# Five pieces of the query-weight gradient, placed by a load count, in a two-block attention backward kernel

## The chip, the cores and the metric

The kernel runs on one core of one Trainium2 chip. The metric is the device time of one execution in microseconds (us). A core has a matrix engine (TensorE, PE in the profile, its weight loads PEld), a vector engine (VectorE, DVE), a scalar engine (ScalarE, ACT), GpSimd (POOL), SyncE (SP), which issues all DMAs here, and 16 DMA engines. Matmuls write to PSUM, which the kernel uses as eight banks of 128 x 2 KB; VectorE or ScalarE copies ("evacuates") a bank to SBUF.

## The reference

Two attention blocks, A and B, each with its own x, caches and weights; the output is their results side by side, and all gradients for a given grad_out are returned too.

```
B, Sq, D = 8, 96, 640;  H, Sk, Dh = 32, 512, 128          # per block, all bf16
q = (x @ wq) by heads;  p = softmax(q @ k_cache^T * Dh**-0.5)
o = p @ v_cache;        out = o.reshape(B, Sq, H*Dh) @ wo
return concat(out_A, out_B), and by vjp: dx, dk_cache, dv_cache, dwq, dwo of each block
```

## The kernel before

**Ticks.** Block A's 32 heads come first, then block B's. One tick is one (head, batch) pair: 8 ticks a head, 256 a block, 512 in all. Each (head, batch) pair goes through eight steps, each one or two ticks behind the other (table OFF), so one tick holds a step of each of several pairs: scores into S_ps and their row maximum negm on VectorE (L298, L300), the exponential E_sb on ScalarE (L310), the normalised P_sb on GpSimd (L329), its transpose PT_sb, the output and its copy into OD (L359 to L378), dV (L389), dP and dl (L417, L419), dS on VectorE (L421), dK (L432), and the transposes of dS and dQ (L340, L346). OD holds, for seven heads, the transposed output OT_h and the transposed query gradient dQT_h.

**Work once a head.** Beside that each head has pieces of its own, put into ticks by the table HK, counted from the head's first tick: pB at -3 (transposes of wo and wq), pC at -2 to 0 (Q and dO), pD at 1 and 2 (their transposes), qA0 at 18 (transposes the output into Onat; evacuated by ScalarE), qA1 at 17 (transposes dQ into dQnat; by VectorE), qB at 19 and 20 (two halves of dwo), and qD. qD computes dwq for two heads at a time, so it runs for odd heads alone: D is cut into DC = 5 chunks of 128 rows, and each chunk is six matmuls of 256 columns over the tokens (L490) from dQnat, which holds the dQ of both heads. Before, two chunks lie in tick 18, two in tick 19 and one in tick 21 of the odd head, counted from that head's first tick, and qD_st stores the result one tick after the last. dQnat and dwq_sb have one buffer each.

**Work once a group.** After every 5 (or 4, or 2) heads, gU multiplies their outputs by wo, and their dQ by wq (o_ps, L514), spread over some 15 ticks. Ticks of other heads have none.

**What sets the order.** An Emitter collects (tick, slot, function) and calls the functions sorted by tick, slot and order of adding. Within a tick the loads come first (slots 0 to 2), then the steps of the pairs, then the work of the heads (SL_HEAD, 90), then the groups' (95). qD is added at SL_HEAD + 2, so behind qA, pD (90) and qB (91) of its tick. A framework orders the instructions of each engine once, at build time, from this order as a priority (the scores, the exponential and the normalisation get a higher one), and sets the semaphores. Each engine then runs its instructions in that order. All PSUM tiles share one pool of eight banks (tag "bank"): whoever allocates waits until an earlier tile's evacuation is done. DMAs that are pinned stay in the order in which they were emitted.

```
HK = dict(pA=-10, pA2=-9, pB=-3, ..., qA0=18, qA1=17, qB=[19, 20], qD=[(18, 0, 2), (19, 2, 4), (21, 4, 5)])
for (k_, c_lo, c_hi) in hk["qD"]:
    if c_lo < DC and h % 2 == 1:
        em.add(c0t + k_, SL_HEAD + 2, qD(h, c_lo, min(c_hi, DC)))
```

In an odd head's count, the following even head's ticks 17, 18, 19, 20 and 21 are 25, 26, 27, 28 and 29.

Of the kernel before, what the change touches and what calls it, by code (L numbers as in the profile page):

```python
# [15 lines left out]
class Emitter:  # L16
    def __init__(self):
        self.items = []
        self.n = 0

    def add(self, tick, slot, fn):
        self.items.append((tick, slot, self.n, fn))
        self.n += 1

    def run(self):
        self.items.sort(key=lambda x: (x[0], x[1], x[2]))
# [14 lines left out]
SL_HEAD = 90  # L41
SL_GRP = 95
SL_SETUP = 96

OFF = dict(ldk=-5, ldv=-4, kt=-3, vt=0, s2=3, s3=3, s4=4, s5=5, s6=6, s7=7, s8=8)
HK = dict(pA=-10, pA2=-9, pB=-3, pC0=[-2, 0], pC1=[-1, 0], pD1=1, pD0=2, qA0=18, qA1=17, qB=[19, 20], qD=[(18, 0, 2), (19, 2, 4), (21, 4, 5)])
EV = dict(pB0="act", pB1="dve", pC00="act", pC01="act", pC10="act", pC11="dve", pD0="dve", pD1="dve", qA0="act", qA1="dve", qB0="act", qB1="dve", qD="dve", gU="act")
GSPREAD0 = 9
PRIO_OFF = 2000
GSPREAD1 = 9  # L50
SLOTS = dict(LOAD=0, S2A=5, S2B=5.5, S1=6, S8=10, S7=20, S5=30, S4=40, S6=50, S3A=52, S3B=53, S5B=54, HEAD=SL_HEAD, GRP=SL_GRP)
# [2 lines left out]
def build_block(tc, em, tick0, blk, x, kc, vc, wq, wo, g_all, out_all, dx, dk, dv, dwq, dwo, ident, ones, pools, HG=6, first=True, groups=None):  # L54
    nc = tc.nc
    B, Sq, D = x.shape
    _, H, Sk, Dh = kc.shape
# [4 lines left out]
    DC = D // 128  # L62
# [142 lines left out]
    def pB(h):  # L205
        def f():
            st = HS[(blk, h)]
            woT_ps = bank([128, DC * 128], BF16, "woT_ps")
            for c in range(DC):
                nc.tensor.transpose(woT_ps[:, c * 128:(c + 1) * 128], st["wo_h"][:, c * 128:(c + 1) * 128], ident[:])  # L210
            woT_h = hd.tile([128, DC * 128], BF16, name="woT_h", bufs=1)
            evac(EV["pB0"], woT_h[:], woT_ps[:])
            st["woT_h"] = woT_h
            wqT_ps = bank([128, DC * 128], BF16, "wqT_ps")
            for c in range(DC):
                nc.tensor.transpose(wqT_ps[:, c * 128:(c + 1) * 128], st["wq_h"][:, c, :], ident[:])
            wqT_h = hst.tile([128, D], BF16, name="wqT_h")
            evac(EV["pB1"], wqT_h[:], wqT_ps[:])
            st["wqT_h"] = wqT_h
            st["slot"] = (blk * H + h) % OD.shape[2]  # L220
            st["OT_h"] = OD[:, 0, st["slot"]]
            st["dQT_h"] = OD[:, 1, st["slot"]]
            st["QT_h"] = hd.tile([128, T], BF16, name="QT_h")
            st["dOT_h"] = hd.tile([128, T], BF16, name="dOT_h")
        return f

    def pC(h, which, si):
        def f():
            st = HS[(blk, h)]
            (t0, w) = tsplits[si]  # L230
            if which == 0:
                dst = st["QT_h"]
                lhs = lambda c: st["wq_h"][:, c, :]
                rhsT = S["xT"]
                sc = scale
            else:
                dst = st["dOT_h"]
                lhs = lambda c: st["woT_h"][:, c * 128:(c + 1) * 128]
                rhsT = S["gT"]
                sc = None  # L240
            q_ps = bank([128, w], F32, "q_ps")
            for c in range(DC):
                nc.tensor.matmul(q_ps[:], lhs(c), rhsT[:, c, t0:t0 + w], start=(c == 0), stop=(c == DC - 1))  # L243
            evac(EV["pC%d%d" % (which, si)], dst[:, t0:t0 + w], q_ps[:], sc)
        return f
# [34 lines left out]
    def c_s1(h, b):  # L280
        def f():
            st = CS[(blk, h, b)]
            kT_ps = bank([128, Sk], BF16, "kT_ps")
            for c in range(KC):
                nc.tensor.transpose(kT_ps[:, c * 128:(c + 1) * 128], st["K_sb"][:, c, :], ident[:])
            KT = wk.tile([128, Sk], BF16, name="KT_pe", bufs=1)
            nc.vector.tensor_copy(KT[:], kT_ps[:])
            st["KT"] = KT[:]
        return f
# [211 lines left out]
    gsplits = dsplits  # L501
# [58 lines left out]
    for g in range(NG):  # L560
        h0 = GH0[g]
        for hh in range(groups[g]):
            h = h0 + hh
            c0t = tick0 + h * B
            if not (first and h == 0):
                em.add(c0t + HK["pA"], SLOTS["LOAD"] + 1.7, pA(h))
                em.add(c0t + HK["pA2"], SLOTS["LOAD"] + 1.7, pA2(h))
            em.add(c0t + HK["pB"], SL_HEAD, pB(h))
            fh = first and h == 0
            p0, p1, d1, d0, late = HK["pC0"], HK["pC1"], HK["pD1"], HK["pD0"], 0  # L570
            if fh:
                p1, d1, d0, late = [3, 3], 3, 4, 7
            elif h == 0:
                p0, p1, d1, d0, late = [-2, 2], [0, 3], 3, 4, 7
            for si in range(NTS):
                em.add(c0t + p0[min(si, 1)], SL_HEAD, pC(h, 0, si))
                em.add(c0t + p1[min(si, 1)], SL_HEAD + late, pC(h, 1, si))
            em.add(c0t + d1, SL_HEAD + (8 if late else 0), pD(h, 1))
            em.add(c0t + d0, SL_HEAD, pD(h, 0))
            for b in range(B):  # L580
                ct = c0t + b
                if b % NB == 0:
                    em.add(tick0 - 12 if first and h == 0 and b == 0 else ct + OFF["ldk"], SLOTS["LOAD"], c_ld(h, b, "K", 7))
                    em.add(ct + OFF["ldv"], SLOTS["LOAD"], c_ld(h, b, "V", 6))
                    if not k_on_pe(h, b):
                        em.add(ct + OFF["kt"], SLOTS["LOAD"] + 1, c_xt(h, b, "KT", 4))
                    em.add(ct + OFF["vt"], SLOTS["LOAD"] + 1, c_xt(h, b, "VT", 4))
                if k_on_pe(h, b):
                    em.add(ct + 2, SLOTS["S1"], c_s1(h, b))
                em.add(ct + OFF["s2"], SLOTS["S2A"], c_s2a(h, b))  # L590
                em.add(ct + OFF["s2"], SLOTS["S2B"], c_s2b(h, b))
                em.add(ct + OFF["s3"], SLOTS["S3A"], c_s3a(h, b))
                em.add(ct + OFF["s3"], SLOTS["S3B"], c_s3b(h, b))
                em.add(ct + OFF["s5"], SLOTS["S5B"], c_s5b(h, b))
                if b % 2 == 1:
                    em.add(ct + OFF["s4"] + 1, SLOTS["LOAD"] + 1.5, c_st(h, b, "v"))
                    em.add(ct + OFF["s7"] + 1, SLOTS["LOAD"] + 1.5, c_st(h, b, "k"))
                em.add(ct + OFF["s4"], SLOTS["S4"], c_s4(h, b))
                for i, o in enumerate(("s8", "s7", "s5", "s4")):
                    SX.setdefault(ct + OFF[o], [None] * 4)[i] = (blk, h, b)  # L600
                em.add(ct + OFF["s6"], SLOTS["S6"], c_s6(h, b))
                em.add(ct + OFF["s7"], SLOTS["S7"], c_s7(h, b))
            hk = HK if first or h < H - 1 else dict(HK, qA0=13, qB=[14, 15], qA1=16, qD=[(19, 0, 2), (19, 2, 4), (19, 4, 5)])
            em.add(c0t + hk["qA0"], SL_HEAD, qA(h, 0))
            for di in range(len(wsplits)):
                em.add(c0t + hk["qB"][di], SL_HEAD + 1, qB(h, di))
            em.add(c0t + hk["qB"][-1] + 1, SLOTS["LOAD"] + 1.6, qB_st(h))
            em.add(c0t + hk["qA1"], SL_HEAD, qA(h, 1))
            for (k_, c_lo, c_hi) in hk["qD"]:
                if c_lo < DC and h % 2 == 1:  # L610
                    em.add(c0t + k_, SL_HEAD + 2, qD(h, c_lo, min(c_hi, DC)))
            if h % 2 == 1:
                em.add(c0t + hk["qD"][-1][0] + 1, SLOTS["LOAD"] + 1.6, qD_st(h))
        cLg = tick0 + (h0 + groups[g] - 1) * B + B - 1
        gs0 = max(3, (GSPREAD0 * groups[g]) // HG)
        gs1 = max(3, (GSPREAD1 * groups[g]) // HG)
        if not first and g == NG - 2:
            gs0, gs1 = 9, 9
        if g == 0:
            em.add(cLg + OFF["s5"] - 2, SL_LOAD, setup_acc)  # L620
        subs = [(0, t, gi) for t in range(TT) for gi in range(len(gsplits))] + [(1, t, gi) for t in range(TT) for gi in range(len(gsplits))]
        n_out = TT * len(gsplits)
        for i, (which, t, gi) in enumerate(subs):
            if which == 0:
                tk = cLg + OFF["s5"] + 2 + (i * gs0) // n_out
            else:
                tk = cLg + OFF["s8"] + 2 + gs0 - 3 + ((i - n_out) * gs1) // n_out
            em.add(tk, SL_GRP, gU(g, which, t, gi))
            if g == NG - 1 and gi == len(gsplits) - 1:
                em.add(tk + 1, SLOTS["LOAD"] + 1.6, gU_st(which, t))  # L630
    pools["c_s45"] = c_s45
    pools["c_s8"] = c_s8
    return tick0 + H * B
# [121 lines left out]
```

## Time and profile before

| | |
|---|---|
| time, median of 3 runs | 1643.09 us (1642.14 to 1643.6) |
| the profiled execution's own time | 1643.09 us |
| its span, first to last instruction | 1641.3 us |
| granted TensorE clock, mean | 1.000 |
| DMA traffic | 454.96 MB, mean 277 GB/s |

How to read it: the profile is of one execution. "Busy" of an engine is the time in which an instruction of it is under way; matmuls are pipelined, and their ends are modelled, so TensorE's busy time is not TensorE at its peak, and two matmuls that follow at once overlap in the rows. A row of the groups has the line, the engine, the operation, out<-in with shapes and the count, then the busy time and the mean of one in ns, then the engine's idle time just before and what ended it. A row of the timeline has the start and the duration in us, and in square brackets the idle time before it with what ended it. A row of the stretches has, for each engine, the busy time and in brackets the number of instructions, then the granted clock, the DMA share and GB/s.

### The profile page before, as it was taken

Reading aid. Unit: us, or ns where it says so; the run is one execution under the profiler, and the core shown is the slowest. Engines: PE = TensorE matmul, PEld = TensorE weight load, DVE = VectorE, ACT = ScalarE, POOL = GpSimd, SP = SyncE. Lnnn points to the kernel's source line nnn. Section 1 sums busy time; section 2 is a strip of 40 time slices with the busy share of each in tenths; the row PEclk is TensorE's granted clock in tenths of the full one; section 3 lists DMA queues with packets and bytes.
Section 4 is the critical chain, followed back from the end, with each engine's and each line's share of the span. In section 5 each row is a group of like instructions: output and inputs, shape, how many; then the busy total and the mean of one; then the engine's idle time right before and its main releaser. Section 6 shows DMA issues by size and latency. Waiting matters only on the chain.

```text
span 1641.3 us, 55280 instructions
## 1 busy us (share of the span) xinstructions
PE 1621.3 (99%) x21048; PEld 1289.1 (79%) x21048; DVE 1268.2 (77%) x2856; ACT 1388.7 (85%) x3518; POOL 526.7 (32%) x1034
## 2 busy tenths in 40 slices
PE   8999999999999999999999999999999999999999
PEld 7887787787787787877878877877877877877876
DVE  6886677778787787788878867878778778777777
ACT  7999897898798797988869998978977978987975
POOL 2333232333233232333323332323322322332332
PEclk9999999999999999999999999999999999999999
DMA  9999999999999999999999999999999999999994
GB/s 266 289 282 294 269 291 291 271 271 292 260 272 293 279 274 271 264 281 285 297 284 292 293 289 279 284 298 260 291 291 258 280 277 282 283 292 259 281 276 146
DMA packets 875626, 454.96 MB, mean 277 GB/s; under 512 B 548192, under 2 KB 875360, under 8 KB 875360
## 3 DMA queue, kind: packets, MB, share of 16 engines
q1 hardware_dynamic: 875360, 451.43, 112.4%
q8 instruction: 165, 2.70, 0.7%
q14 instruction: 101, 0.83, 0.1%
HBM read 161.09 MB, written 159.12 MB: 195 GB/s over the span
## 4 chain that ended last, share of the span: by engine, by line
PE 81%; ACT 10%; DVE 4%; issue 3%; DMA 2%; SPq 0%; POOL 0%; ACTq 0%; DVEq 0%; POOLq 0%
PE q_ps L243 13%; PE o_ps L514 12%; PE dwq_ps L490 6%; PE dP_ps L417 6%; PE dK_ps L432 6%; PE dV_ps L389 5%; PE S_ps L298 5%; PE dst_ps L346 5%; PE dwo_ps L469 4%; PE x_ps L365 4%; PE x_ps L359 4%; PE x_ps L340 4%; ACT E_sb L310 3%; ACT dK_sb L435 2%; PE n_ps L258 2%
## 5 line engine op out<-in xcount | busy, mean ns | idle before, releaser
L329 POOL TENSOR_SCALAR P_sb<-E_sb,rinv 96x512 bf16<-96x512 bf16 x512 | 352.5, 689 | 1087.9 <-DVE rinv L320 1053.6
L310 ACT ACTIVATE E_sb<-S_ps,negm 96x512 bf16<-96x512 f32 x512 | 354.8, 693 | 119.2 <-DVE negm L300 116.8
L421 DVE SCALAR_TENSOR_TENSOR dS_sb<-dP_ps,dl_ps,P_sb 96x512 bf16<-96x512 f32 x512 | 383.6, 749 | 48.9 <-PE dl_ps L419 40.2
L435 ACT ACTIVATE dK_sb<-dK_ps 128x512 bf16<-128x512 f32 x512 | 306.9, 599 | 97.5 <-PE dK_ps L432 96.5
L300 DVE TENSOR_REDUCE negm<-S_ps 96x1 f32<-96x512 f32 x512 | 347.7, 679 | 44.3 <-PE S_ps L298 42.1
L392 ACT ACTIVATE dV_sb<-dV_ps 128x512 bf16<-128x512 f32 x512 | 315.8, 617 | 0.0
L378 ACT ACTIVATE PT_sb<-x_ps 128x384 bf16<-128x384 bf16 x512 | 257.5, 503 | 0.0
L514 PEld LDWEIGHTS <-OD 128*128 128x128 bf16 x1536 | 135.7, 98 | 103.3 <-issue 1.3
L389 PE MATMUL dV_ps<-dOnat_h,P_sb 96*128 96x128 bf16 x2048 | 197.9, 219 | 0.6 <-DVE dOnat_h L160 0.6
L432 PE MATMUL dK_ps<-Qnat_h,dS_sb 96*128 96x128 bf16 x2048 | 197.8, 219 | 0.0
L417 PE MATMUL dP_ps<-VT,dOT_h 128*96 128x512 bf16 x512 | 195.4, 382 | 0.7
L298 PE MATMUL S_ps<-KT,QT_h 128*96 128x512 bf16 x488 | 184.7, 379 | 3.9 <-ACT E_sb L310 2.7
L407 POOL TENSOR_TENSOR prod<-OD,dOT_h 128x96 bf16<-128x96 bf16 x512 | 185.6, 362 | 8.8 <-ACT OD L375 8.2
L348 DVE COPY dST_sb<-dst_ps 128x384 bf16<-128x384 bf16 x512 | 177.2, 346 | 14.0 <-PE dst_ps L346 13.2
L320 DVE RECIPROCAL rinv<-rowsum 96x1 f32<-96x1 f32 x512 | 80.0, 156 | 138.8 <-ACT E_sb L310 134.8
L346 PE MATMUL dst_ps<-ident,dS_sb 96*128 96x96 bf16 x2048 | 171.8, 206 | 4.3 <-ACT PT_sb L378 3.6
L375 ACT ACTIVATE OD<-x_ps 128x192 bf16<-128x192 f32 (+1 forms) x515 | 172.5, 335 | 3.4 <-PE x_ps L340 3.4
L359 PE MATMUL x_ps<-PT_sb,V_sb 128*128 128x96 bf16 x2048 | 172.2, 206 | 0.5 <-ACT PT_sb L378 0.5
L365 PE MATMUL x_ps<-ident,P_sb 96*128 96x96 bf16 x2048 | 171.7, 205 | 0.6 <-POOL P_sb L329 0.3
L340 PE MATMUL x_ps<-dST_sb,K_sb 128*128 128x96 bf16 x2048 | 170.7, 206 | 0.0
L340 PEld LDWEIGHTS <-K_sb 128*128 128x128 bf16 x2048 | 133.7, 98 | 37.1
L514 PE MATMUL o_ps<-wo_h,OD 128*128 128x128 bf16 (+1 forms) x768 | 141.0, 299 | 0.0
(75 smaller groups left out, 3051.9 us busy)
## 6 DMA issues: line engine op xcount, KB each, us to landing
out_dram<-dV_sb SPq DMA_DIRECT2D x256, 256.0 KB, 3.9
out_dram<-dK_sb SPq DMA_DIRECT2D x256, 256.0 KB, 3.6
K_sb<-in_A_k_cache_dram SPq DMA_DIRECT2D x128, 256.0 KB, 4.1
V_sb<-in_A_v_cache_dram SPq DMA_DIRECT2D x128, 256.0 KB, 4.1
K_sb<-in_B_k_cache_dram SPq DMA_DIRECT2D x128, 256.0 KB, 4.2
V_sb<-in_B_v_cache_dram SPq DMA_DIRECT2D x128, 256.0 KB, 4.0
out_dram<-dwo_sb SPq DMA_DIRECT2D x64, 160.0 KB, 3.2
out_dram<-dwq_sb SPq DMA_DIRECT2D x32, 320.0 KB, 3.8
```

The lines of the kernel that those rows point to most:

```text
L298: nc.tensor.matmul(S_ps[:], hs["QT_h"][:, tok], st["KT"], start=True, stop=True)
L300: nc.vector.tensor_reduce(negm[:], S_ps[:], axis=AX.X, op=ALU.max, negate=True)
L310: nc.scalar.activation(E_sb[:], st["S_ps"][:], ACT.Exp, bias=st["negm"][:], scale=1.0, accum_out=rowsum[:])
L329: pinned(nc.gpsimd.tensor_scalar(P_sb[:], st["E_sb"][:], st["rinv"][:], 0.0, op0=ALU.mult, op1=ALU.add))
L340: nc.tensor.matmul(dQT_ps, st["K_sb"][:, c, :], st["dST_sb"][:, c * Sq:(c + 1) * Sq], start=(c == 0), stop=(c == KC - 1))
L389: nc.tensor.matmul(dV_ps[:, c * 128:(c + 1) * 128], P_sb[:, c * 128:(c + 1) * 128], hs["dOnat_h"][:, b * 128:(b + 1) * 128], start=True, s ...
L392: nc.scalar.activation(SB[(blk, h, b // 2, "v")][:, b % 2], dV_ps[:], ACT.Identity, scale=1.0)
L417: nc.tensor.matmul(dP_ps[:], hs["dOT_h"][:, tok], st["VT"], start=True, stop=True)
L421: nc.vector.scalar_tensor_tensor(dS_sb[:], dP_ps[:], dl_ps[:, 0:1], st["P_sb"][:], op0=ALU.subtract, op1=ALU.mult)
L432: nc.tensor.matmul(dK_ps[:, c * 128:(c + 1) * 128], dS_sb[:, c * 128:(c + 1) * 128], hs["Qnat_h"][:, b * 128:(b + 1) * 128], start=True, s ...
L435: nc.scalar.activation(SB[(blk, h, b // 2, "k")][:, b % 2], dK_ps[:], ACT.Identity, scale=1.0)
L514: nc.tensor.matmul(o_ps[:], src[:, t * 128:(t + 1) * 128], rhs, start=(hh == 0), stop=(hh == groups[g] - 1))
```

## The change

Three things change.

- **dwq in pieces of one chunk.** For every odd head but the last of a block, the five chunks of dwq are placed one by one into ticks 18 to 29 of the odd head, at most two in a tick. Two in the same tick form one piece with one evacuation.
- **A load count.** The Emitter's add takes an estimate of the TensorE and ScalarE time (ns) of the work once a head and once a group, and keeps for each tick the sum of TensorE's less 0.8 of ScalarE's. Each chunk goes to the tick whose sum is the smallest so far, and adds 655 to it. The steps of the (head, batch) pairs are in no count, being the same in every tick.
- **dQ of a pair's first head later.** qA1 of the even heads moves from tick 17 to 21 (tick 29 of the odd head before), at SL_HEAD + 3, behind a piece of dwq in the same tick, as dQnat has one buffer.

The last pair of a block keeps its places for dwq. The number of matmuls, their shapes and the data moved stay the same.

```
+        self.load = {}
-    def add(self, tick, slot, fn):
+    def add(self, tick, slot, fn, pe=0, act=0):
         self.items.append((tick, slot, self.n, fn))
         self.n += 1
+        self.load[tick] = self.load.get(tick, 0.0) + pe - ACT_SHARE * act
...
-HK = dict(..., qA0=18, qA1=17, qB=[19, 20], qD=[(18, 0, 2), (19, 2, 4), (21, 4, 5)])
+HK = dict(..., qA0=18, qA1=17, qA1e=21, qDw=(18, 29), qB=[19, 20], qD=[(18, 0, 2), (19, 2, 4), (21, 4, 5)])
+ACT_SHARE = 0.8
...
+            em.add(c0t + HK["pB"], SL_HEAD, pB(h), pe=558, act=713)
...
+                em.add(c0t + p0[min(si, 1)], SL_HEAD, pC(h, 0, si), pe=1090 if si == 0 else 546, act=522 if si == 0 else 420)
+                em.add(c0t + p1[min(si, 1)], SL_HEAD + late, pC(h, 1, si), pe=1090 if si == 0 else 546, act=621 if si == 0 else 0)
+            em.add(c0t + d1, SL_HEAD + (8 if late else 0), pD(h, 1), pe=446)
+            em.add(c0t + d0, SL_HEAD, pD(h, 0), pe=446)
...
+                    em.add(ct + 2, SLOTS["S1"], c_s1(h, b), pe=223)
...
+            em.add(c0t + hk["qA0"], SL_HEAD, qA(h, 0), pe=335, act=820)
             for di in range(len(wsplits)):
+                em.add(c0t + hk["qB"][di], SL_HEAD + 1, qB(h, di), pe=815, act=443 if di == 0 else 0)
-            em.add(c0t + hk["qA1"], SL_HEAD, qA(h, 1))
-            for (k_, c_lo, c_hi) in hk["qD"]:
-                if c_lo < DC and h % 2 == 1:
-                    em.add(c0t + k_, SL_HEAD + 2, qD(h, c_lo, min(c_hi, DC)))
-            if h % 2 == 1:
+            em.add(c0t + (hk["qA1"] if h % 2 == 1 else HK["qA1e"]), SL_HEAD + (0 if h % 2 == 1 else 3), qA(h, 1), pe=335)
+            if h == H - 1:
+                for (k_, c_lo, c_hi) in hk["qD"]:
+                    em.add(c0t + k_, SL_HEAD + 2, qD(h, c_lo, min(c_hi, DC)), pe=655 * (c_hi - c_lo))
                 em.add(c0t + hk["qD"][-1][0] + 1, SLOTS["LOAD"] + 1.6, qD_st(h))
...
+            em.add(tk, SL_GRP, gU(g, which, t, gi), pe=groups[g] * gsplits[gi][1] / 2.4, act=440 if g == 0 else 0)
...
+    for h in range(1, H - 1, 2):
+        c0t = tick0 + h * B
+        ticks = []
+        for _ in range(DC):
+            k_ = min((k for k in range(HK["qDw"][0], HK["qDw"][1] + 1) if ticks.count(k) < 2), key=lambda k: em.load.get(c0t + k, 0.0))
+            em.load[c0t + k_] = em.load.get(c0t + k_, 0.0) + 655
+            ticks.append(k_)
+        ticks.sort()
+        for k_ in sorted(set(ticks)):
+            em.add(c0t + k_, SL_HEAD + 2, qD(h, ticks.index(k_), ticks.index(k_) + ticks.count(k_)))
+        em.add(c0t + ticks[-1] + 1, SLOTS["LOAD"] + 1.6, qD_st(h))
```

More of the change, by code (lines that the diff above doesn't have):

```diff
@@ L45 @@
 OFF = dict(ldk=-5, ldv=-4, kt=-3, vt=0, s2=3, s3=3, s4=4, s5=5, s6=6, s7=7, s8=8)
-HK = dict(pA=-10, pA2=-9, pB=-3, pC0=[-2, 0], pC1=[-1, 0], pD1=1, pD0=2, qA0=18, qA1=17, qB=[19, 20], qD=[(18, 0, 2), (19, 2, 4), (21, 4, 5)])
+HK = dict(pA=-10, pA2=-9, pB=-3, pC0=[-2, 0], pC1=[-1, 0], pD1=1, pD0=2, qA0=18, qA1=17, qA1e=21, qDw=(18, 29), qB=[19, 20], qD=[(18, 0, 2), (19, 2, 4), (21, 4, 5)])
 EV = dict(pB0="act", pB1="dve", pC00="act", pC01="act", pC10="act", pC11="dve", pD0="dve", pD1="dve", qA0="act", qA1="dve", qB0="act", qB1="dve", qD="dve", gU="act")
 GSPREAD0 = 9
+ACT_SHARE = 0.8
 PRIO_OFF = 2000
@@ L567, in build_block @@
                 em.add(c0t + HK["pA2"], SLOTS["LOAD"] + 1.7, pA2(h))
-            em.add(c0t + HK["pB"], SL_HEAD, pB(h))
+            em.add(c0t + HK["pB"], SL_HEAD, pB(h), pe=558, act=713)
             fh = first and h == 0
@@ L575, in build_block @@
             for si in range(NTS):
[L576 to L579, printed above, removed]
+                em.add(c0t + p0[min(si, 1)], SL_HEAD, pC(h, 0, si), pe=1090 if si == 0 else 546, act=522 if si == 0 else 420)
+                em.add(c0t + p1[min(si, 1)], SL_HEAD + late, pC(h, 1, si), pe=1090 if si == 0 else 546, act=621 if si == 0 else 0)
+            em.add(c0t + d1, SL_HEAD + (8 if late else 0), pD(h, 1), pe=446)
+            em.add(c0t + d0, SL_HEAD, pD(h, 0), pe=446)
             for b in range(B):
@@ L588, in build_block @@
                 if k_on_pe(h, b):
-                    em.add(ct + 2, SLOTS["S1"], c_s1(h, b))
+                    em.add(ct + 2, SLOTS["S1"], c_s1(h, b), pe=223)
                 em.add(ct + OFF["s2"], SLOTS["S2A"], c_s2a(h, b))
@@ L603, in build_block @@
             hk = HK if first or h < H - 1 else dict(HK, qA0=13, qB=[14, 15], qA1=16, qD=[(19, 0, 2), (19, 2, 4), (19, 4, 5)])
-            em.add(c0t + hk["qA0"], SL_HEAD, qA(h, 0))
+            em.add(c0t + hk["qA0"], SL_HEAD, qA(h, 0), pe=335, act=820)
             for di in range(len(wsplits)):
-                em.add(c0t + hk["qB"][di], SL_HEAD + 1, qB(h, di))
+                em.add(c0t + hk["qB"][di], SL_HEAD + 1, qB(h, di), pe=815, act=443 if di == 0 else 0)
             em.add(c0t + hk["qB"][-1] + 1, SLOTS["LOAD"] + 1.6, qB_st(h))
-            em.add(c0t + hk["qA1"], SL_HEAD, qA(h, 1))
-            for (k_, c_lo, c_hi) in hk["qD"]:
-                if c_lo < DC and h % 2 == 1:
-                    em.add(c0t + k_, SL_HEAD + 2, qD(h, c_lo, min(c_hi, DC)))
-            if h % 2 == 1:
+            em.add(c0t + (hk["qA1"] if h % 2 == 1 else HK["qA1e"]), SL_HEAD + (0 if h % 2 == 1 else 3), qA(h, 1), pe=335)
+            if h == H - 1:
+                for (k_, c_lo, c_hi) in hk["qD"]:
+                    em.add(c0t + k_, SL_HEAD + 2, qD(h, c_lo, min(c_hi, DC)), pe=655 * (c_hi - c_lo))
                 em.add(c0t + hk["qD"][-1][0] + 1, SLOTS["LOAD"] + 1.6, qD_st(h))
@@ L627, in build_block @@
                 tk = cLg + OFF["s8"] + 2 + gs0 - 3 + ((i - n_out) * gs1) // n_out
-            em.add(tk, SL_GRP, gU(g, which, t, gi))
+            em.add(tk, SL_GRP, gU(g, which, t, gi), pe=groups[g] * gsplits[gi][1] / 2.4, act=440 if g == 0 else 0)
             if g == NG - 1 and gi == len(gsplits) - 1:
                 em.add(tk + 1, SLOTS["LOAD"] + 1.6, gU_st(which, t))
+    for h in range(1, H - 1, 2):
[9 more added lines that the diff above has]
+        em.add(c0t + ticks[-1] + 1, SLOTS["LOAD"] + 1.6, qD_st(h))
     pools["c_s45"] = c_s45
```

## The prediction

> **What bounds the kernel now.** I read the page first: its busy shares, the clock and the chain.
>
> ```profile
> span 1641.3 us, 55280 instructions
> PE 1621.3 (99%) x21048; PEld 1289.1 (79%) x21048; DVE 1268.2 (77%) x2856; ACT 1388.7 (85%) x3518; POOL 526.7 (32%) x1034
> PEclk9999999999999999999999999999999999999999
> PE 81%; ACT 10%; DVE 4%; issue 3%; DMA 2%; SPq 0%; POOL 0%; ACTq 0%; DVEq 0%; POOLq 0%
> ```
>
> TensorE is busy for 1621.3 of 1641.3 us at an undisturbed clock, and the chain of work that ended last is 81% TensorE and 10% ScalarE. The change takes no matmul away, so it can win only time in which TensorE stands still. The view "who waited for whom" shows little of that:
>
> ```profile
> engine line waited for: us in total, times, longest us
> ACT E_sb L310 <- DVE negm L300: 116.8, 190, 2.1
> ...
> DVE dwq_sb L162 <- PE dwq_ps L490: 43.9, 73, 1.4
> ...
> PE dst_ps L346 <- ACT PT_sb L378: 3.6, 21, 0.2
> PE S_ps L298 <- ACT E_sb L310: 2.7, 17, 0.2
> ...
> PE S_ps L298 <- DMA KT<-K_sb: 0.8, 2, 0.6
> ```
>
> Two repeated TensorE waits, both for ScalarE: 21 and 17 times. Their 3.6 and 2.7 us are too small, because a matmul's modelled end hangs over the next one's start. What they cost is seen by comparing ticks with equal TensorE work. I count ticks from the first tick of a pair's odd head, as the table HK does. The stretches below are ticks 18, 19, 20, 21, 25, 26, 27, 28 and 29 of one pair that has no o_ps work in them (head 21 of the first block), each from one first L340 matmul to the next.
>
> ```profile
> core 0: us, PE busy (x) PEld busy (x) DVE busy (x) ACT busy (x) POOL busy (x), PEclk, DMA share, GB/s
> 577.75:581.54 3.79, 3.79 (x57) 3.42 (x55) 3.79 (x8) 3.53 (x9) 1.27 (x3) 1.00 1.12 278
> 581.54:585.26 3.72, 3.72 (x48) 3.15 (x46) 2.58 (x6) 2.94 (x8) 1.02 (x2) 1.00 1.40 316
> 585.26:587.66 2.40, 2.40 (x35) 1.99 (x33) 1.83 (x5) 2.19 (x6) 1.04 (x2) 1.00 0.77 237
> 587.66:590.47 2.81, 2.81 (x46) 2.54 (x43) 2.57 (x7) 2.24 (x7) 1.02 (x2) 1.00 1.06 305
> 598.49:600.87 2.38, 2.38 (x44) 2.19 (x41) 2.00 (x6) 2.38 (x8) 0.81 (x2) 1.00 1.08 316
> 600.87:603.44 2.57, 2.57 (x45) 2.32 (x43) 2.57 (x7) 2.42 (x8) 1.14 (x3) 1.00 1.14 306
> 603.44:606.16 2.72, 2.56 (x36) 1.98 (x35) 2.41 (x7) 2.72 (x8) 0.89 (x2) 1.00 1.30 187
> 606.16:608.57 2.41, 2.41 (x35) 1.99 (x33) 1.65 (x5) 2.41 (x8) 0.88 (x3) 1.00 1.16 347
> 608.57:610.72 2.15, 2.15 (x39) 1.94 (x37) 1.91 (x6) 2.15 (x7) 0.84 (x3) 1.00 1.23 260
> ```
>
> Ticks 25 and 26 hold the same TensorE work (one pD and one qA beside the eight steps of every tick), but take 2.38 and 2.57 us: 0.19 is lost in tick 26. Ticks 27 and 28 each hold half of dwo, and take 2.72 and 2.41: 0.31 is lost in tick 27. In tick 27 ScalarE is busy for the whole 2.72 us. Ticks 18 and 19, with the same other work as 26 and 27, are the long ones, since most of dwq lies there; there ScalarE is idle for 0.26 and 0.78 us. So dwq now sits where TensorE is already the later one, and is missing where ScalarE is. The timeline shows the two waits, and ScalarE's reason for them:
>
> ```profile
> 603.44 0.33 PE L340 MATMUL x_ps<-dST_sb,K_sb 128*128 128x96 bf16 x4
> ...
> 603.61 0.34 PE L346 MATMUL dst_ps<-ident,dS_sb 96*128 96x96 bf16 x4
> ...
> 603.74 0.82 ACT L157 ACTIVATE Onat<-nat_ps 128x768 bf16<-128x768 bf16 x1
> ...
> 604.43 0.70 ACT L310 ACTIVATE E_sb<-S_ps,negm 96x512 bf16<-96x512 f32 x1
> ...
> 605.27 0.38 PE L298 MATMUL S_ps<-KT,QT_h 128*96 128x512 bf16 x1 [0.16 <-ACT E_sb L310]
> ...
> 610.72 0.33 PE L340 MATMUL x_ps<-dST_sb,K_sb 128*128 128x96 bf16 x4
> ...
> 611.23 0.33 PE L346 MATMUL dst_ps<-ident,dS_sb 96*128 96x96 bf16 x4 [0.17 <-ACT PT_sb L378]
> ```
>
> In tick 27, S_ps waits for the bank that E_sb has to free, and E_sb stands behind the evacuation of Onat, which holds ScalarE for 0.69 us (603.74 to 604.43). At the start of tick 30, dst_ps comes 0.51 us after x_ps (610.72 to 611.23), where 0.17 is the rule (603.44 to 603.61): 0.34 is lost.
>
> **The change, part by part.** *Where the pieces go.* The planner's load of a tick is TensorE less 0.8 of ScalarE, from the costs in the diff. Without o_ps work, tick 21 has 558 - 0.8 x 713 = -12; ticks 18 and 26 have 446 + 335 - 0.8 x 820 = 125; tick 29 has -12 + 335 = 323, with dQ of the even head now in it; tick 25 has 446; ticks 19 and 27 have 815 - 0.8 x 443 = 461. A piece adds 655, so the five go to 18, 21, 25, 26 and 29. I worked the rule through all 30 pairs with the group sizes (5,5,5,5,4,4,4 and 5,5,5,5,5,5,2): 12 pairs get just these ticks. In 5 more o_ps fills ticks 18 to 23, and the pieces lie at 25, 26, 27, 29 and one of 23 and 24. In 2 pairs they lie at 20, 27, 28 and twice at 29. In the other 11 o_ps fills most of the window, or the block ends.
>
> *What a piece is worth.* Its six matmuls take 6 x 1.31 / 12 = 0.655 us, by
>
> ```profile
> 174.81 1.31 PE dwq_ps L490 x12
> ...
> L162 DVE TENSOR_SCALAR dwq_sb<-dwq_ps 128x512 bf16<-128x512 f32 x64 | 44.3, 692 | 40.0 <-PE dwq_ps L490 40.0
> ...
> L160 DVE COPY dQnat<-nat_ps 128x768 bf16<-128x768 bf16 x64 | 34.8, 544 | 0.0
> ...
> L162 DVE TENSOR_SCALAR dwq_sb<-dwq_ps 128x256 bf16<-128x256 f32 x32 | 13.3, 416 | 3.9 <-PE dwq_ps L490 3.9
> ```
>
> That is more than any one of the three losses. A piece at 25 covers the 0.19 of tick 26, one at 26 the 0.31 of tick 27, one at 29 the 0.34 of tick 30. The first two are won in 12 + 5 = 17 pairs (S_ps waited 17 times): 17 x 0.50 = 8.5 us. The third is won in 12 + 5 + 2 = 19 of the 21 times: 19 x 0.34 = 6.5 us. Together 15.0 us.
>
> *What the old places lose.* In the 12 pairs tick 18 keeps one chunk of two, and tick 19 none: 3.72 - 1.31 = 2.41 us, the length of tick 28. Tick 18 then stands as tick 26 does, so the chunk covers tick 19's E_sb as well. Bounds: 0, if the cover holds, to 12 x 0.31 = 3.7 us, if tick 19 loses what tick 27 does today. In the 5 pairs ticks 18 to 21 lose all of dwq, but have o_ps; between 0 and 5 x 0.50 = 2.5 us by the same rows. Below nothing isn't excluded: a shift can undo small waits in the 11 other pairs, which I bound by the same 0.31 a pair, 3.4 us, with either sign. I take 3 us of loss in all, about half of 6.2, since a cover just over the loss need not hold everywhere.
>
> *ScalarE's room.* From tick 18 through 29 the pair takes 32.97 us, and ScalarE is busy for 31.00:
>
> ```profile
> 577.75:610.72 32.97, 32.81 (x463) 27.65 (x462) 27.15 (x61) 31.00 (x81) 11.85 (x24) 1.00 1.16 284
> ```
>
> With 0.50 us gone 32.47 are left: ScalarE fits, with 1.5 us to spare, but at 95%. So not much beyond the covered waits can be won.
>
> *VectorE.* By my count the 150 chunks need 9 double and 132 single evacuations, for 60 and 30 now: 9 x 0.692 + 132 x 0.416 - 60 x 0.692 - 30 x 0.416 = 7.1 us more, on an engine at 77%. The cover is its idle time of 373 us; what may not hide is where they stand in its queue (the first rival). The copy of the even head's dQnat, 0.544 us, moves from tick 25 to 29, where VectorE is busy for 1.91 of 2.15 us; with one chunk's evacuation that is 1.91 + 0.42 + 0.54 = 2.87, and TensorE's tick becomes 2.15 + 0.655 + 0.335 = 3.14. It stays below.
>
> *Waits added, and queues.* dQnat has one buffer, so the even head's copy must follow the last piece. It is emitted behind it in the same tick, and TensorE's own order serves that: no new wait. The store of dwq is still issued one tick after the last piece, now up to tick 30 for 22. On SyncE's queue it then stands ahead of the weight loads of tick 30, which are due in ten ticks' time, and behind that tick's K and V loads. The dwq_sb buffer is written again at tick 34 at the earliest, four ticks of over 2 us after the store; a store lands in 3.8:
>
> ```profile
> out_dram<-dwq_sb SPq DMA_DIRECT2D x32, 320.0 KB, 3.8
> ```
>
> Cost nothing. Bytes stay; TensorE waited for a late KT twice, 0.8 us in all.
>
> *The sum.* 15.0 - 3 = 12 us. The profiled execution took 1643.1 us, 1.8 above its span, and that is the median of the runs too: 1643.1 - 12 = 1631 us, 0.7%. The forecast's own range is 1625 (all covered, nothing lost at the old places, 3.4 won elsewhere) to 1638 (6.2 us lost at the old places, and 3.4 elsewhere).
>
> **A rule on buffers.** Both repeated waits are for a PSUM bank: S_ps for E_sb's, dst_ps for PT_sb's. The Trainium skill, "Perfetto Trace Analysis", section Identifying Dependency Chains, says that a gap that repeats on the engine which should be saturated can mean that there isn't enough SBUF or PSUM for the next tile. The rows bear it out that far, but show the bank held by a late ScalarE, rather than too few banks. By that rule five smaller pieces, each with a bank of its own, would make it worse, and the time would be the third rival's rather than the forecast's.
>
> **The rivals.** *First, slower: VectorE's queue.* An evacuation of dwq_ps waits at the head of VectorE's queue, and negm and so E_sb stand behind it. Tick 19 shows it:
>
> ```profile
> 585.04 0.68 ACT L310 ACTIVATE E_sb<-S_ps,negm 96x512 bf16<-96x512 f32 x1 [0.67 <-DVE negm L300]
> ...
> 585.46 0.69 DVE L162 TENSOR_SCALAR dwq_sb<-dwq_ps 128x512 bf16<-128x512 f32 x1 [0.51 <-PE dwq_ps L490]
> ```
>
> Now that falls where ScalarE has time. By the planner's rule 23 + 18 + 21 = 62 pieces come to ticks 25, 26 and 29, where it has none. If each holds E_sb up by 0.4 us (between 0 and 0.67), ScalarE loses 25 us where 15 are won: 10 us slower, 1653. It decides from 15 / 62 = 0.24 us a piece. For it: VectorE waited 73 times for dwq_ps. Against it: in these rows negm came before the evacuation, and E_sb waited since ScalarE had nothing else; a late ScalarE doesn't.
>
> *Second: half of it.* The waits come back at ticks 19 and 20, as ScalarE is at 95%: 15 - 8 = 7 us, 1636.
>
> *Third: banks.* 141 evacuations for 90 are 51 more turns of a bank; if each costs one wait of 0.3 us, 15 us are lost for 15 won: 1643. The same time comes out if the framework's scheduler lays the matmuls of a piece behind the wait that it should cover, so that the change does not do what it says.
>
> **How the numbers follow.** Forecast 0.60 at 1631; half of it 0.08; banks or order 0.12; VectorE's queue 0.20. About 0.2%, 3.3 us, is what a measurement of this kernel can tell from no change. Faster by more than that: 0.60 + 0.08 = 0.68; within: 0.12; slower: 0.20. The range reaches from 1623, somewhat below the forecast's own, to 1650, which takes in most of the slower case.
>
> **What would show it.** Right: the 17 waits of S_ps for E_sb and the 21 of dst_ps for PT_sb nearly gone; ticks 26 and 27 without loss (3.02 and 2.40 us); ScalarE's busy share up to about 85.3% with equal work; the evacuations of dwq_ps counted as 134 of 256 columns and 13 of 512 (with the 2 and 4 of the blocks' last pairs). Wrong: E_sb waiting for negm longer than 116.8 us in all, at ticks 25, 26 and 29; the waits of S_ps standing at tick 19 instead; or new TensorE waits on banks that dwq_sb frees.

## The result, and the profile after

| | before | changed |
|---|---|---|
| time, median | 1642.80 us (4 runs, 1642.14 to 1643.60) | 1629.64 us (4 runs, 1627.36 to 1630.68) |
| ratio, 95% interval | | 0.9917 (0.9905 to 0.9929) |
| span of the profiled execution | 1641.3 us | 1628.0 us |

The changed kernel is 0.83% faster; 12 us were forecast, and the span is 13.3 us shorter. The page of the changed kernel (its line numbers are 3 higher; 167 matmul records are missing from this trace, so TensorE's busy time reads too small):

```profile
span 1628.0 us, 55048 instructions
PE 1605.0 (99%) x20881; PEld 1286.4 (79%) x21048; DVE 1269.9 (78%) x2907; ACT 1391.5 (85%) x3518; POOL 528.5 (32%) x1034
PE 93%; DVE 2%; ACT 2%; issue 1%; DMA 1%; SPq 0%; POOL 0%; DVEq 0%; ACTq 0%; POOLq 0%
```

The work is the same, and the chain that ended last is now TensorE's for 93% instead of 81%, ScalarE's for 2% instead of 10%. Who waited for whom, changed kernel (total us, times, longest):

```profile
ACT E_sb L313 <- DVE negm L303: 111.7, 191, 2.1
...
DVE dwq_sb L165 <- PE dwq_ps L493: 25.1, 43, 1.4
...
DVE dwq_sb L165 <- DMA out_dram<-dwq_sb: 2.5, 1, 2.5
...
PE dwo_ps L472 <- DVE dwq_sb L165: 2.2, 1, 2.2
...
PE dst_ps L349 <- ACT PT_sb L381: 0.3, 1, 0.3
```

The 17 waits of S_ps for E_sb are gone, and of the 21 of dst_ps for PT_sb one is left. E_sb does not wait longer for negm than before (111.7 us against 116.8). One new wait has come: an evacuation of dwq waited 2.5 us for a store, and TensorE 2.2 us for the bank that it frees; such a wait is one of the prediction's signs of being wrong. The same pair's ticks 18, 19, 20, 21, 25, 26, 27, 28 and 29 (head 21 of the first block) as stretches of the changed kernel:

```profile
core 0: us, PE busy (x) PEld busy (x) DVE busy (x) ACT busy (x) POOL busy (x), PEclk, DMA share, GB/s
572.60:575.73 3.13, 3.13 (x50) 2.83 (x49) 3.13 (x8) 2.99 (x9) 1.28 (x3) 1.00 1.32 194
575.73:578.14 2.41, 2.41 (x36) 1.99 (x34) 2.10 (x7) 2.20 (x6) 0.57 (x1) 1.00 1.16 347
578.14:580.54 2.40, 2.40 (x35) 1.99 (x33) 1.58 (x5) 2.40 (x8) 0.87 (x3) 1.00 1.47 187
580.54:583.45 2.91, 2.91 (x45) 2.60 (x43) 2.67 (x8) 2.91 (x8) 1.60 (x4) 1.00 0.87 257
591.48:594.19 2.71, 2.71 (x43) 2.44 (x41) 2.30 (x6) 2.71 (x9) 1.08 (x3) 1.00 1.15 353
594.19:597.22 3.03, 3.03 (x49) 2.76 (x47) 2.72 (x7) 2.39 (x7) 1.24 (x3) 1.00 1.16 334
597.22:599.63 2.41, 2.41 (x35) 1.99 (x33) 2.09 (x7) 2.41 (x7) 0.53 (x1) 1.00 1.17 301
599.63:602.04 2.41, 2.41 (x36) 1.99 (x34) 1.55 (x5) 2.41 (x8) 0.88 (x3) 1.00 1.32 188
602.04:605.32 3.28, 3.28 (x52) 2.94 (x50) 3.04 (x9) 3.28 (x10) 1.67 (x4) 1.00 1.19 304
```

Ticks 27 and 28 are now equal (2.41), as are 19 and 20; tick 26 takes 3.03 where 3.02 was worked out. Tick 29 takes 3.28 where 3.14 was, so 0.14 is lost there, and tick 21, with the same work as before, 2.91 instead of 2.81. Over all sixteen ticks of a pair without o_ps (head 11 of the second block), before and then changed:

```profile
1138.48:1182.39 43.91, 43.54 (x606) 36.18 (x605) 34.87 (x80) 41.94 (x110) 16.11 (x32) 1.00 1.16 283
```

```profile
1130.82:1173.93 43.11, 43.00 (x603) 35.99 (x604) 34.91 (x82) 41.92 (x110) 16.29 (x33) 1.00 1.18 277
```

That is 0.80 us a pair. Summed over the pairs, each from the first L340 matmul (L343 in the changed kernel) of its tick 18 to that of its tick 34, worked out from the two traces:

| pairs | before, us | changed, us | difference |
|---|---|---|---|
| the 12 with pieces at 18, 21, 25, 26, 29 | 555.4 | 546.4 | -9.0 |
| the 5 with 25, 26, 27, 29 and one more | 250.7 | 246.0 | -4.7 |
| the 2 with two pieces at 29 | 105.1 | 104.1 | -1.0 |
| head 3 of the second block | 54.5 | 58.1 | +3.6 |
| 9 others (the last pair before the kernel's end left out) | 494.0 | 491.7 | -2.3 |

The evacuations came out as counted:

```profile
L165 DVE TENSOR_SCALAR dwq_sb<-dwq_ps 128x256 bf16<-128x256 f32 x134 | 55.7, 416 | 21.4 <-PE dwq_ps L493 17.9 <-DMA out_dram<-dwq_sb 2.5 <-DMA out_dram<-dV_sb 0.7
...
L165 DVE TENSOR_SCALAR dwq_sb<-dwq_ps 128x512 bf16<-128x512 f32 x13 | 9.0, 692 | 7.1 <-PE dwq_ps L493 7.1
```

### The profile page after: what moved, and what is told of

Same layout as the page of the kernel before. It is cut to its first block, busy times and chain, and to the rows that moved or that the text cites. A ratio compares the mean times of both kernels' runs of the same rounds, so it can differ in the third digit from the quotient of the medians.

```text
span 1628.0 us, 55048 instructions
## 1 busy us (share of the span) xinstructions
PE 1605.0 (99%) x20881; PEld 1286.4 (79%) x21048; DVE 1269.9 (78%) x2907; ACT 1391.5 (85%) x3518; POOL 528.5 (32%) x1034
## 4 chain that ended last, share of the span: by engine, by line
PE 93%; DVE 2%; ACT 2%; issue 1%; DMA 1%; SPq 0%; POOL 0%; DVEq 0%; ACTq 0%; POOLq 0%
PE q_ps L246 13%; PE o_ps L517 12%; PE dK_ps L435 7%; PE dV_ps L392 7%; PE dP_ps L420 7%; PE S_ps L301 7%; PE dwo_ps L472 6%; PE dwq_ps L493 6%; PE dst_ps L349 5%; PE x_ps L368 5%; PE x_ps L362 5%; PE x_ps L343 5%; PE n_ps L261 3%; PE nat_ps L458 3%; PE woT_ps L213 1%
## 5 line engine op out<-in xcount | busy, mean ns | idle before, releaser
L313 ACT ACTIVATE E_sb<-S_ps,negm 96x512 bf16<-96x512 f32 x512 | 356.3, 696 | 117.2 <-DVE negm L303 111.7
L343 PE MATMUL x_ps<-dST_sb,K_sb 128*128 128x96 bf16 x2048 | 170.9, 206 | 0.0
L343 PEld LDWEIGHTS <-K_sb 128*128 128x128 bf16 x2048 | 135.3, 98 | 38.2
L493 PE MATMUL dwq_ps<-dQnat,x_nat 128*128 128x256 bf16 x960 | 142.7, 273 | 0.0
```

The lines of the kernel that those rows point to most:

```text
L313: nc.scalar.activation(E_sb[:], st["S_ps"][:], ACT.Exp, bias=st["negm"][:], scale=1.0, accum_out=rowsum[:])
L343: nc.tensor.matmul(dQT_ps, st["K_sb"][:, c, :], st["dST_sb"][:, c * Sq:(c + 1) * Sq], start=(c == 0), stop=(c == KC - 1))
```

## The experiments

Each was compared with runs of the kernel before on its own chip; ratios to it, with 95% intervals.

| kernel | median, us | ratio |
|---|---|---|
| late transposes alone | 1643.94 | 0.9998 (0.9989 to 1.0007) |
| split in place | 1644.69 | 1.0002 (0.9994 to 1.0011) |
| one chunk at 25 | 1644.98 | 1.0006 (0.9997 to 1.0015) |
| one chunk at 26 | 1636.63 | 0.9955 (0.9942 to 0.9967) |
| one chunk at 29 | 1640.86 | 0.9983 (0.9974 to 0.9992) |
| fixed ticks | 1634.92 | 0.9944 (0.9932 to 0.9956) |
| no ScalarE share | 1630.65 | 0.9912 (0.9897 to 0.9927) |
| tick 25 barred | 1633.22 | 0.9934 (0.9922 to 0.9947) |
| store given time | 1632.13 | 0.9924 (0.9911 to 0.9936) |
| other groups in block B | 1632.17 | 0.9927 (0.9913 to 0.9941) |
| Onat by VectorE, on before | 1642.52 | 0.9990 (0.9981 to 0.9999) |
| Onat by VectorE, on changed | 1638.24 | 0.9961 (0.9949 to 0.9973) |

**Split in place.** One part of the change alone: five pieces, old ticks.

```
-HK = dict(..., qD=[(18, 0, 2), (19, 2, 4), (21, 4, 5)])
+HK = dict(..., qD=[(18, 0, 1), (18, 1, 2), (19, 2, 3), (19, 3, 4), (21, 4, 5)])
```

> The kernel before with dwq in five pieces of one chunk, each with a bank and an evacuation of its own, but at the old ticks (18, 18, 19, 19, 21). Theory of the cover: nothing moves to the late ticks, so the waits there stay (17 of S_ps for E_sb, 21 of dst_ps for PT_sb): 1643 us, within 2 us. Rival, banks: 60 more turns of a bank at 0.3 us a wait: up to 1661 us. Rival, shorter evacuations free VectorE earlier and that is the gain: about 1632 us.

No change, and the waits of this kernel are the old ones, to the count:

```profile
ACT E_sb L310 <- DVE negm L300: 137.2, 198, 2.1
...
PE dst_ps L346 <- ACT PT_sb L378: 3.6, 21, 0.2
PE S_ps L298 <- ACT E_sb L310: 2.7, 17, 0.2
```

So neither the smaller evacuations nor the further turns of a bank (62 in the trace) matter. The gain is in the places. E_sb waits for negm for 137.2 us in all here, 20 more than before, at no cost: that total alone says little of the time.

**Late transposes alone.** The other part alone.

```
-em.add(c0t + hk["qA1"], SL_HEAD, qA(h, 1))
+em.add(c0t + (hk["qA1"] if h % 2 == 1 else 21), SL_HEAD + (0 if h % 2 == 1 else 3), qA(h, 1))
```

> The kernel before with one part of the change alone: dQ of the even heads is transposed at tick 21 (the odd head's 29); dwq stays at ticks 18, 19 and 21. Theory (TensorE work covers ScalarE's lag wherever it is put): tick 25 loses 0.33 us of TensorE work, so the wait in tick 26 grows from 0.2 by up to 0.33 us in 17 pairs (+5.6 us); tick 29 gains 0.33, so the wait of dst_ps for PT_sb in tick 30 (0.34 us, 21 times) goes (-6.5 us). Net -1 us: 1642 us, with the 21 waits gone and those of tick 26 longer. Rival (this move is the source of the gain): about 1630 us.

The net is nothing, as expected, and of the 21 waits one is left. But the time did not go back to tick 26. Its ticks 28 and 29 (head 11 of the second block):

```profile
1166.33:1168.91 2.58, 2.58 (x35) 2.05 (x33) 1.43 (x5) 2.58 (x9) 1.28 (x3) 1.00 1.10 254
1168.91:1171.82 2.91, 2.88 (x46) 2.40 (x44) 2.67 (x7) 2.91 (x9) 1.60 (x4) 1.00 1.01 210
```

Tick 28 took 2.41 before and takes 2.58; tick 29, with 2.15 + 0.335 = 2.49 of work, takes 2.91. ScalarE is busy throughout. Ticks 26 to 30 are one stretch in which ScalarE is behind: less TensorE work ahead of it only lets the wait come elsewhere. In this pair ticks 25 to 30 take 15.52 us, 0.30 more than before, and tick 33 takes 0.20 less.

**One chunk moved**, on top of the late transposes, from tick 19 to 25, 26 or 29, for all pairs alike but the last of a block.

```
-HK = dict(..., qD=[(18, 0, 2), (19, 2, 4), (21, 4, 5)])
+HK = dict(..., qD=[(18, 0, 2), (19, 2, 3), (21, 3, 4), (25, 4, 5)])     # or 26, or 29
...
```

> The kernel before, with dQ of the even heads at tick 21 (29 of the odd head) and one chunk of dwq taken from tick 19 to tick 25 (18 twice, 19, 21, 25); no load count, every pair alike. Theory: the chunk covers the wait in tick 26, which without dQ in tick 25 is 0.2 to 0.5 us, and may leave TensorE late enough for a part of tick 27's too; tick 27's 0.31 us mostly stays. Against the kernel with the late transposes alone: 17 x 0.2 to 0.5 = 3 to 9 us less.

> As the last, with the one chunk at tick 26. Theory: the 17 waits of S_ps for E_sb in tick 27 go (17 x 0.31 = 5.3 us), the wait in tick 26, which lies before the chunk, stays: 5 us less than with the late transposes alone.

> As the last, with the one chunk at tick 29. Theory: tick 30's wait is already covered by the transposes of dQ, so nothing more is won: the time of the kernel with the late transposes alone, within 2 us. Rival (a chunk at 29 is worth 0.34 us in 19 pairs): 6.5 us less.

The sums over ticks 25 to 30 of the same pair (head 11 of the second block): late transposes alone, then with the chunk at 25, 26 and 29.

```profile
sum 15.52, PE 15.43 PEld 12.47 DVE 13.11 ACT 15.40 POOL 6.06; mean PE 2.57 PEld 2.08 DVE 2.18 ACT 2.57 POOL 1.01
```

```profile
sum 16.17, PE 15.96 PEld 12.98 DVE 13.47 ACT 15.42 POOL 6.09; mean PE 2.66 PEld 2.16 DVE 2.25 ACT 2.57 POOL 1.02
```

```profile
sum 15.66, PE 15.63 PEld 12.96 DVE 13.68 ACT 15.59 POOL 6.08; mean PE 2.60 PEld 2.16 DVE 2.28 ACT 2.60 POOL 1.01
```

```profile
sum 15.88, PE 15.84 PEld 13.01 DVE 13.55 ACT 15.59 POOL 6.15; mean PE 2.64 PEld 2.17 DVE 2.26 ACT 2.60 POOL 1.02
```

A chunk that covers nothing makes 15.52 + 0.655 = 16.18. At 25 it is 16.17: nothing covered on balance. At 26, 15.66: 0.52 covered. At 29, 15.88: 0.30 covered (0.15 in pairs that have o_ps in tick 30). With the chunk at 25, tick 26 no longer loses its 0.2 us (2.37 for 2.58), but the time comes back at ticks 27 and 29 (2.68 and 3.02 us for 2.58 and 2.91). That loss is ahead of Onat: with the late transposes alone PT_sb ends at 1161.51, and dst_ps starts then, 0.34 us after x_ps, at the start of tick 26, while Onat's evacuation begins at 1164.32. So ScalarE is behind before it takes Onat, other than the corrected theory of the next experiment has it. The ACT figures tell why: ScalarE is busy for 15.42 of 16.17, so it was idle for 0.75. The row of E_sb in tick 26 of that kernel, and the one in the changed kernel:

```profile
1163.55 0.68 ACT L310 ACTIVATE E_sb<-S_ps,negm 96x512 bf16<-96x512 f32 x1 [0.75 <-DVE negm L300]
```

```profile
595.11 0.68 ACT L313 ACTIVATE E_sb<-S_ps,negm 96x512 bf16<-96x512 f32 x1 [0.64 <-DVE negm L303]
```

That is the whole idle time, and it puts off all that ScalarE has behind it: Onat's evacuation begins 5.85 us after the start of tick 25, where it began after 5.21. The scores, dOnat's copy and negm of tick 25, with the chunk at 25 and then with the late transposes alone:

```profile
1161.87 0.38 PE L298 MATMUL S_ps<-KT,QT_h 128*96 128x512 bf16 x1
...
1162.17 0.68 DVE L160 COPY dOnat_h<-n_ps 96x1024 bf16<-96x1024 bf16 x1
...
1162.77 0.68 DVE L300 TENSOR_REDUCE negm<-S_ps 96x1 f32<-96x512 f32 x1
```

```profile
1160.56 0.38 PE L298 MATMUL S_ps<-KT,QT_h 128*96 128x512 bf16 x1
...
1161.37 0.68 DVE L300 TENSOR_REDUCE negm<-S_ps 96x1 f32<-96x512 f32 x1
...
1161.97 0.68 DVE L160 COPY dOnat_h<-n_ps 96x1024 bf16<-96x1024 bf16 x1
```

With the chunk the scores come 1.96 us after the tick's start instead of 1.45, and VectorE takes dOnat's copy ahead of negm. The scores were done at 1162.25, but negm began at 1162.77: about 0.5 of the 0.75 us is that order. The changed kernel has it too. What a chunk at 25 covers with negm ahead of the copy wasn't tried. All three expectations on the single chunks were wrong in size: 25 won nothing, 26 won 7.3 us (1643.94 to 1636.63, for 5 expected), 29 won 3.1 us between theory and rival.

**Tick 25 barred.** The planner of the changed kernel without that tick.

```
-k_ = min((k for k in ... if ticks.count(k) < 2), ...)
+k_ = min((k for k in ... if k != 25 and ticks.count(k) < 2), ...)
```

> The changed kernel, its planner barred from tick 25. In pairs without o_ps the chunk goes to tick 19 instead. Corrected theory (ScalarE falls behind only once it has Onat, in tick 26; a chunk ahead of that makes ScalarE idle as long as it occupies TensorE, 0.75 us in tick 26 of the run with one chunk at tick 25, and covers nothing on balance): tick 26's 0.2 us come back, tick 29's 0.14 go and ScalarE's idle time in tick 26 goes: the changed kernel's time within 2 us. The prediction's account (a chunk at 25 is worth 0.19 us in 17 pairs): 3 us slower.

0.9934 against 0.9917: the intervals overlap, so the two accounts aren't told apart by the time; the difference, 2.8 us, is nearer to the prediction's 3. In the trace the 0.2 us of tick 26 came back, tick 29's loss fell from 0.14 to 0.04, and tick 21's 0.10 went. Over their sixteen ticks seven of the 12 pairs took the same time as in the changed kernel, within 0.01 us, the other five 0.15 to 1.18 us more, and four of the 5 pairs 0.21 us more. So what tick 25 is worth with the four others in place stays open.

**The planner.** First without ScalarE's term (ACT_SHARE = 0.0), then without the count, all pairs at 18, 21, 25, 26 and 29:

> The changed kernel with ACT_SHARE = 0: the planner counts TensorE's work alone. In a pair without o_ps the loads are then 446 at tick 25, 558 at 21, 781 at 18 and 26, 815 at 19, 893 at 29, so the pieces go to 18, 19, 21, 25 and 26, none to 29. Theory: ticks 26 and 27 stay covered, and tick 30's wait is covered by the transposes of dQ at 29 (0.33 us against 0.34): 1630 to 1633 us. Rival (ScalarE's term is what finds the places): tick 30's 0.34 us comes back in 19 pairs, 6.5 us: 1636 us or more.

> The changed kernel without its load count: all 30 pairs have their chunks at ticks 18, 21, 25, 26 and 29. Theory: the same 17 to 19 pairs win the same; in the other 11 pairs o_ps covers these waits anyway, and a chunk's place matters little: 1630 us, within 3 us of the changed kernel. Rival (the count is needed): the pairs with o_ps lose what they have not lost, 1635 us or more.

By the time, the ScalarE term isn't needed: 0.9912. The rival falls, though its mechanism is there: tick 29, which gets no piece, lost 0.3 us in pairs without o_ps, where the changed kernel lost 0.14. (The profiled execution of this kernel took 1635.19 us, the other three 1629.33 to 1631.25, so its trace shows more loss than is usual.) The count of TensorE's work is needed: fixed ticks gave 0.9944, beyond the changed kernel's interval, a miss for the theory. By the ticks' starts the pair at block A's end (head 29) took 56.2 us instead of 53.9, and the first pair of block B 45.2 instead of 43.4; those two, at the change of blocks, make 4.1 of the 6.6 us by which its span (1634.6 us) is the longer.

**Store given time.** The changed kernel loses 3.6 us in one pair. Its rows: the store of the pair before on SyncE's queue, the evacuation that waits for it, and dwo behind that, for the bank.

```profile
923.50 0.43 SPq L501 DMA_DIRECT2D out_dram<-dwq_sb  x1
```

```profile
927.10 0.42 DVE L165 TENSOR_SCALAR dwq_sb<-dwq_ps 128x256 bf16<-128x256 f32 x1 [2.52 <-DMA out_dram<-dwq_sb]
...
927.58 1.03 PE L472 MATMUL dwo_ps<-g_nat,Onat 128*128 128x320 bf16 x6 [2.15 <-DVE dwq_sb L165]
```

The last chunk lay in the tick that started at 906.8 us, so the store came some 13 us after its due tick; the K and V loads, their transposing DMAs and the stores of dK and dV stood ahead of it on a queue that was late: from 896.9 to 924.0 us SyncE issued one transfer behind the other, with no gap over 0.15 us. The queue was late before the change too: there the same store went out 9.9 us after its tick began (at 908.36 us), and that of the next pair 13.7 us after (at 957.15 us), but with twelve ticks from the store's tick until dwq_sb was written again, and not four. The experiment lets this one pair start at tick 20:

```
-k_ = min((k for k in range(HK["qDw"][0], HK["qDw"][1] + 1) ...), ...)
+k_ = min((k for k in range(HK["qDw"][0] + (2 if h == 3 and not first else 0), HK["qDw"][1] + 1) ...), ...)
```

> The changed kernel, with one pair (head 3 of the second block) allowed ticks 20 to 29 alone, two ticks later than the others. In the changed kernel's trace the first evacuation of that pair waited 2.5 us for the store of the pair before, which SyncE issued some 13 us after its tick, and tick 19 took 6.2 us instead of 2.4. Theory: that wait goes, 3 us less: 1626.5 us, and no wait of dwq_sb for its store. Rival (TensorE would have waited there in any case, as block B's loads are late): no change, 1629.6 us.

No gain. The wait for the store fell to 0.3 us, but one tick later TensorE stood still for a transposed K:

```profile
932.32 0.42 PE L301 MATMUL S_ps<-KT,QT_h 128*96 128x512 bf16 x1 [3.23 <-DMA KT<-K_sb]
```

So the rival holds: block B starts with five heads without o_ps, the faster ticks there ask for data sooner than it comes, and where one wait was avoided here the next one took its place.

**Other groups in block B**, so that o_ps work comes ahead of that place (groupsB = 4, 5, 5, 5, 5, 5, 3):

> The changed kernel with block B's heads in groups of 4, 5, 5, 5, 5, 5, 3 instead of 5, 5, 5, 5, 5, 5, 2: the same matmuls, but block B's first o_ps work starts 8 ticks earlier, at its tick 38, ahead of the place (its tick 43) where the changed kernel and all its variants stop for 2 to 3 us. Theory (the transfers fall behind in the long stretch without o_ps at block B's start, and the changed kernel, being faster there, runs into them): about 5 us of TensorE work ahead of that place let the transfers catch up; the stop and the half clock after it go: 3 to 5 us less than the changed kernel, 1625 us. Rival (the third head more in the last group lengthens the tail): 3 us more at the end, and no gain in sum.

A miss: 0.9927. The rival's longer tail is there: from the start of the last tick to the end of the span it is 17.4 us instead of 14.8. The stop went from its place, and came back 100 us later, in the next long stretch without o_ps:

```profile
1029.60 0.43 DVE L165 TENSOR_SCALAR dwq_sb<-dwq_ps 128x256 bf16<-128x256 f32 x1 [3.62 <-DMA out_dram<-dwq_sb]
```

Whether the transfers' rate, their order on SyncE's queue or the issuing itself sets this is left open; a second dwq_sb buffer, which would free the evacuation, wasn't tried, as the kernel's SBUF has no room for it.

**Onat by VectorE**, which takes its evacuation from ScalarE (EV qA0="dve"), on the kernel before and on the changed one:

> The kernel before, with Onat evacuated by VectorE (about 0.54 us, as dQnat) instead of ScalarE (0.69 us of its time, in ticks 18 and 26); dwq where it was. Theory (ScalarE's lag behind Onat is the cause of all three waits): ScalarE has 0.69 us less in tick 26, the waits there and in tick 27 go, and that in tick 30 shrinks: 17 x 0.5 to 0.85 = 8 to 14 us less, 1629 to 1635 us. Rival (VectorE, which holds negm, is as late as ScalarE was: busy for 2.57 of tick 26's 2.57 us): no gain or slower, 1643 us or more.

> The changed kernel, with Onat evacuated by VectorE and no ScalarE cost counted for it, so the planner sees 781 at ticks 18 and 26. Theory: most of the waits that Onat causes are covered already; what is left is 0.1 to 0.4 us a pair: 0 to 5 us less than the changed kernel. Rival: VectorE, with dwq's evacuations as well, becomes the late one in ticks 18 and 26: slower than the changed kernel by 3 us or more.

Far less than the theory asked for. On the kernel before the 21 and 17 waits nearly went, 3 of the first being left, but the ratio is 0.9990: in head 11 of the second block ticks 25 to 30 take 15.08 us instead of 15.22, and VectorE is busy throughout ticks 26 and 27 (2.57 and 2.59 us), as the rival has it. So to count the waits isn't to price them. E_sb waited 141.0 us for negm instead of 116.8, but so it nearly did in the split in place (137.2), at no cost; which of VectorE's steps holds TensorE up here isn't shown. On the changed kernel it is slower than without (0.9961 against 0.9917). There the planner, which counts no ScalarE time for Onat in this run, also took two pieces of the 12 pairs from ticks 18 and 26 to 19 and 27, so what the places cost and what VectorE costs isn't told apart.

## Why the prediction was right, point by point

- **The bound and the places.** Right, and shown: splitting alone and the late transposes alone are within 0.1% of no change, and one chunk taken from tick 19 to 26 makes more than half of the gain. Of the three late places tried alone, the two from tick 26 on covered something.
- **What each piece is worth.** The sum was right, its parts were not, so that they add up is in part luck. The piece at 25 was credited with 0.19 us; it does end tick 26's loss, but alone it covers nothing on balance, since ScalarE then idles for 0.75 us. The one at 26 was credited with 0.31 and is worth 0.52 on top of the late transposes (0.44 to 0.59 in 16 of the 17 pairs). Tick 30's wait was put down to the piece at 29; the late transposes alone end 20 of the 21 waits and take tick 30 from 3.00 to 2.81 us, and the time shows up at 28 and 29, where the piece then covers 0.30. The failed step is that a wait's price belongs to the tick where it shows: the stretch from tick 26 to 30 has one sum.
- **15.0 us in 19 pairs, 3 lost.** The 19 pairs won 9.0 + 4.7 + 1.0 = 14.7 us net. The old places lost nothing, as in the lower bound: tick 19 takes 2.41. What was lost there instead is 0.14 at tick 29 and 0.10 at tick 21, which the prediction did not have; a 0.2 us wait at tick 33, which it had not seen either, went as well. The 3 us of loss were right in size only: they came from one pair, of whose cause the prediction said "cost nothing".
- **That step, the store's queue**, failed. Four ticks were to suffice for a store of 3.8 us; SyncE's queue was some 13 us late there. The 0.8 us of waits for KT didn't show it, but the trace before did: the stores of dwq went out up to 13.7 us after their ticks began.
- **First rival, VectorE's queue.** At tick 25 E_sb is held up by 0.64 to 0.75 us, beyond the 0.24 a piece from which it would decide. What stands ahead of negm there is dOnat's copy, and not an evacuation of dwq as the rival had it: that one comes behind negm (594.93 us for 594.34 in the changed kernel). At 26 and 29 ScalarE is behind, and in all E_sb waited 111.7 us. It took the worth of one piece in three.
- **Third rival, banks**, and the rule on buffers, as far as more turns of a bank were to cost time: refuted by the split in place, 62 more turns at 1.0002. The waits were for a late ScalarE. The sentence on repeated gaps in the Trainium skill, "Perfetto Trace Analysis", stands in its section Optimization Strategy, just ahead of the section that the prediction names.
- **ScalarE at 95%.** In the pair without o_ps it is busy for 41.92 of 43.11 us, 97%, with equal work. The forecast that little beyond the covered waits could be won held: no kernel tried is clearly faster than the changed one. TensorE's own work leaves as little: what was found lost in that pair is 0.14 us at tick 29 and 0.10 at tick 21.

## What to carry to other kernels

Where two engines are nearly even on average, look for the stretch in which the second one is behind, and put movable work of the first into it: the price of the lag is that of the whole stretch until the second engine has caught up. Work put in just ahead of it can make the second idle instead; see in the rows what then stands ahead of its input. Test the worth of a place by moving one piece alone and comparing the sum over the stretch with the sum plus the piece. And when ticks get shorter, see how late the DMA queue already runs there, by when its stores go out and not only by waits: the next stop was in a place where the trace before showed 0.8 us of waits, but stores that were up to 13.7 us late.

## What the runs showed of the hardware

A stop of TensorE has a second price. After the 2.15 us wait for dwo's bank, the changed kernel's clock was granted at half:

```profile
923.91:927.58 3.67, 1.52 (x29) 1.35 (x26) 1.15 (x4) 2.89 (x7) 0.00 (x0) 1.00 1.15 303
927.58:928.41 0.83, 0.83 (x7) 0.58 (x7) 0.83 (x3) 0.00 (x0) 0.46 (x1) 0.97 1.12 348
928.41:930.11 1.70, 1.70 (x9) 1.08 (x7) 0.79 (x2) 0.48 (x2) 0.57 (x2) 0.50 1.26 251
```

The half clock lasted 3.41 us in the trace's record of the granted clock, so by estimate it cost about 1.7 us of work, on top of the stop. In the traces of this study, counted from the end of one matmul's row to the start of the next, seven stops in mid-run lasted 2.15 us or more (2.15, 2.27, 2.88, 2.96, 3.22, 3.23, 3.26), and each was joined by one such stretch; those of 1.0 to 1.8 us were not, but for one of 1.56 us in the first 8 us of a run. The Trainium skill, "TensorE: Matmul & The Clock Gate", section Why this matters for your kernels, advises against gaps in TensorE's work of over about 3 us; here 2.15 sufficed, so the measurement is the stricter one.
